# All 64x64 products of a step together on TensorE, in a fixed order, with the outputs of a unit one step later

## The chip, the cores and the metric

The kernel runs on one core of one Trainium2 chip. The metric is the device time of one execution in microseconds. A ratio is the mean time of one kernel's fast runs over the mean of the other's fast runs of the same rounds on the same chip, so it is not quite the ratio of the medians that stand beside it.

## The reference

An mLSTM cell, then a multiplicative feed-forward network (FFN), all in fp32. There are 4 batches, 8 heads, 768 steps and a head size of 40. Its recurrence is

```python
C = f_stab * C + i_stab * outer(v_t, k_t);  n = f_stab * n + i_stab * k_t
y_t = sigmoid(o_t) * (C @ q_t) / max(|n . q_t|, 1)
# bridge: x is y as (3072, 320)
out = ((x @ w1) * (x @ w2)) @ w3 @ w_out        # 320 -> 1024 -> 1024 -> 320
```

Both kernels compute the recurrence in blocks. A *unit* is one batch and 128 time steps, that is two halves of 64 steps; there are 24 units. They also fold `w3 @ w_out` into one matrix `w3o` on the way, and convert the weights, which come as 64-bit words, on VectorE.

## The kernel before

For each unit TensorE makes these products (names as in the profile):

- `pt`: k and q transposed, 128x128 transposes that use the full array. ScalarE copies them to `kT` and `qT`.
- `ss`: scores of a half; `pc`: what a half adds to the state; `pi`: what the state gives to the outputs; `ph`: weighted scores times v. These use 64 rows and 64 columns of the array, so up to four run side by side in its quarters.
- `px`: y transposed to `xT`, the input of the FFN.

The FFN has `pa` and `pb` (x times w1 and w2). Its 320 input columns are two blocks of 128 and a *rest* of 64, and the rests of pa and pb run as two 64x128 products. `po` is the output product. `w3p` and `wp` fold w3.

```python
def scores(n):
    ...
    _, ss = two_banks("ss", L)                 # one PSUM buffer of two banks for ss, pc and pi in turn
    for p in range(NP):
        for hip, x in ((0, 0), (1, 1), (0, 1), (1, 0)):
            nc.tensor.matmul(ss[t, hip, p, :], lhsT=kT[r, p, t], rhs=qT[r, p, t], ...)
    nc.vector.tensor_tensor(out=pv, in0=ss, in1=pv, op=OP.mult)          # pw
def cell(n):                                   # one step after scores(n)
    ...                                        # pc; two states; pi; h; ph; h; den; o_in; y
    nc.gpsimd.tensor_copy(out=y_t[n][:, DM:DM + REM], in_=y_t[n][:, KF * P:DM])
for s in ...:                                  # program order; the scheduler may move instructions
    turn(s)                                    # pt
    ffn_up(first); scores(s); convert(...); cell(s - 1)
    ffn_up(others); x_trans(s - 2); ffn_out(...)          # px stands near the end of the step
```

The scheduler that builds the instruction streams may change the order of independent products on TensorE, and does.

## Time and profile before

| | before |
|---|---|
| median, fastest, slowest | 549.59, 548.06, 551.09 us (4 runs) |
| profiled span | 545.3 us |
| mean granted TensorE clock (share of full speed) | 0.978 |
| TensorE busy | 92% |

### The profile page before, as it was taken

The page shows a single profiled execution, that of the slowest core. Times are in us where ns is not written, and L with a number is a line of the kernel's source. Part 1 is how long each engine was busy: PE and PEld are TensorE (multiplying, and loading weights), DVE is VectorE, ACT ScalarE, POOL GpSimd, SP SyncE. Part 2 cuts the span into 40 slices and gives each one's busy share as a digit, 9 for nine tenths or more (in the row PEclk, how much of TensorE's full clock was granted, in tenths as well). Part 3 has the DMA queues.
Part 4 walks back from the last instruction along what each step waited for, and adds up shares of the span by engine and source line. Part 5 has one row for each costly group of instructions (what it writes and reads, how often), then busy time and mean ns, then how long its engine had stood idle before and what let it go on. Part 6 is the DMA issues. An engine that isn't in the chain of part 4 may idle for free.

```text
span 545.3 us, 11006 instructions
## 1 busy us (share of the span) xinstructions
PE 500.7 (92%) x4538; PEld 302.7 (56%) x4538; DVE 231.9 (43%) x500; ACT 174.2 (32%) x419; POOL 88.0 (16%) x157
## 2 busy tenths in 40 slices
PE   4647989896999998999989999999999999999997
PEld 3535666674555554555556665556555455353675
DVE  7856779895655654655613202331232100101000
ACT  3636655854343154143153213212110111111100
POOL 2432343241212212212101302200000000000000
PEclk9966999999999999999989999999999999999999
DMA  8698999987224355222232213200000000000011
GB/s 172 134 168 187 172 198 178 199 203 167 63 72 133 85 99 133 70 66 57 37 69 57 68 39 68 44 13 14 13 1 25 0 24 25 0 24 1 24 37 37
DMA packets 113042, 43.32 MB, mean 79 GB/s; under 512 B 102304, under 2 KB 105504, under 8 KB 112992
## 3 DMA queue, kind: packets, MB, share of 16 engines
q1 hardware_dynamic: 112992, 42.61, 35.8%
q8 instruction: 36, 0.59, 0.5%
q14 instruction: 14, 0.11, 0.1%
HBM read 38.57 MB, written 4.03 MB: 78 GB/s over the span
## 4 chain that ended last, share of the span: by engine, by line
PE 68%; DVE 2%; ACT 2%; DMA 2%; issue 2%; SPq 0%; POOL 0%; DVEq 0%; ACTq 0%; POOLq 0%
PE po L435 19%; PE pa L424 13%; PE pb L424 12%; PE pa L427 7%; PE wp L209 7%; PE ph L291 2%; PE pc L263 2%; PE pt L231 2%; PE pi L284 2%; PE px L314 1%; DVE pw L244 1%; PE ss L242 1%; ACT a_sb L429 1%; DMA raw<-in_moe_w_dram 1%; DMA pw<-U_rest 1%
## 5 line engine op out<-in xcount | busy, mean ns | idle before, releaser
L430 DVE TENSOR_TENSOR ab<-pb,a_sb 128x512 f32<-128x512 f32 (+1 forms) x56 | 34.3, 613 | 204.3 <-ACT a_sb L429 135.6
L435 PE MATMUL po<-w3o,ab 128*128 128x320 f32 x384 | 105.8, 433 | 0.0
L424 PE MATMUL pa<-xT,w 128*128 128x512 f32 (+1 forms) x224 | 99.4, 557 | 3.6 <-ACT xT L315 3.6
L424 PE MATMUL pb<-xT,w 128*128 128x512 f32 (+1 forms) x224 | 94.4, 541 | 0.5 <-DVE w L153 0.5
L435 PEld LDWEIGHTS po<-w3o,ab 128*128 128x128 f32 x384 | 72.0, 190 | 30.1 <-issue 1.5
L222 ACT ACTIVATE pw<-pw,aT 128x64 f32<-128x64 f32 x192 | 52.9, 341 | 55.7 <-DMA pw<-U_rest 42.5
L429 ACT ACTIVATE a_sb<-pa 128x512 f32<-128x512 f32 (+1 forms) x56 | 29.8, 532 | 126.8 <-PE pb L427 125.4
L424 PEld LDWEIGHTS pb<-xT,w 128*128 128x128 f32 x224 | 41.5, 191 | 36.1 <-issue 32.3
L427 PE MATMUL pa<-xT,wr 64*128 64x512 f32 (+1 forms) x112 | 56.0, 580 | 0.2 <-DVE wr L153 0.2
L427 PE MATMUL pb<-xT,wr 64*128 64x512 f32 (+1 forms) x112 | 56.0, 580 | 0.0
L424 PEld LDWEIGHTS pa<-xT,w 128*128 128x128 f32 x224 | 37.5, 190 | 30.8 <-issue 23.9
L258 POOL TENSOR_TENSOR vw<-vbuf,wT 128x328 f32<-128x328 f32 x24 | 22.1, 920 | 156.7 <-PE pc L263 87.3
L224 POOL TENSOR_SCALAR_AFFINE_SELECT pw<-pw 64x512 f32<-64x512 f32 x48 | 34.4, 718 | 59.3 <-ACT pw L222 57.7
L438 ACT COPY o_sb<-po 128x320 f32<-128x320 f32 x24 | 10.2, 426 | 87.1 <-PE po L435 84.5
L209 PE MATMUL wp<-wo,w3T 128*128 128x320 f32 x128 | 37.7, 449 | 0.3
L427 PEld LDWEIGHTS pa<-xT,wr 64*128 64x128 f32 x112 | 16.5, 184 | 35.3 <-issue 34.7
L209 PEld LDWEIGHTS wp<-wo,w3T 128*128 128x128 f32 x128 | 24.3, 195 | 10.5 <-DVE w3T L203 1.1
L291 PE MATMUL ph<-vbuf,pw 64*64 64x41 f32 x768 | 29.9, 233 | 0.0
L291 PEld LDWEIGHTS ph<-vbuf,pw 64*64 64x64 f32 x768 | 27.3, 142 | 1.6 <-issue 0.5
L263 PEld LDWEIGHTS pc<-vw,kbuf 64*64 64x64 f32 x704 | 15.5, 146 | 21.9 <-DVE pw L244 15.9
L148 ACT ACTIVATE raw<-raw 128x512 f32<-128x512 f32 (+1 forms) x34 | 21.4, 631 | 19.6 <-DMA raw<-in_moe_w_dram 19.6
L263 PE MATMUL pc<-vw,kbuf 64*64 64x41 f32 x704 | 19.3, 242 | 8.3 <-DVE pw L244 8.3
(78 smaller groups left out, 503.4 us busy)
## 6 DMA issues: line engine op xcount, KB each, us to landing
raw<-in_moe_w_dram SPq DMA_DIRECT2D x24, 512.0 KB, 4.6
pw<-U_rest SPq DMA_DIRECT2D x40, 128.0 KB, 3.7
kbuf<-in_k_dram SPq DMA_DIRECT2D x24, 160.0 KB, 4.2
qbuf<-in_q_dram SPq DMA_DIRECT2D x24, 160.0 KB, 4.4
vbuf<-in_v_dram SPq DMA_DIRECT2D x24, 160.0 KB, 3.8
o_in<-in_o_gate_dram SPq DMA_DIRECT2D x24, 160.0 KB, 3.7
out_dram<-o_sb SPq DMA_DIRECT2D x24, 160.0 KB, 1.8
raw<-in_moe_w_out_dram SPq DMA_DIRECT2D x8, 320.0 KB, 4.0
```

The costliest lines, as they stand in the source:

```text
L148: nc.scalar.mul(out=hi.bitcast(FP), in_=hi.bitcast(FP), mul=2.0 ** -111)
L209: nc.tensor.matmul(wp, lhsT=w3T[:, ki, :], rhs=wo[:, ki, :], start=(ki == 0), stop=(ki == FO - 1))
L222: nc.scalar.activation(out=pw[:, h, :], in_=pw[:, h, :], func=AF.Exp, bias=aT[:, c, b * H + h:b * H + h + 1])
L224: nc.gpsimd.affine_select(out=pw[r], in_=pw[r], compare_op=OP.is_ge, fill=0.0, base=0, pattern=[[0, H], [1, L]], channel_multiplier=-1)
L258: nc.gpsimd.tensor_tensor(out=vw, in0=vt, in1=wT[:, c, hs].unsqueeze(2).to_broadcast([P, H, D1]), op=OP.mult)
L263: nc.tensor.matmul(pc[halves[e], x, p, :], lhsT=kt[halves[x], 2 * p + e, :], rhs=vw[halves[x], 2 * p + e, :], start=True, stop=True)
L291: nc.tensor.matmul(ph[r, hd, :], lhsT=pw[r, hd, :], rhs=vt[r, hd, :], start=True, stop=True)
L424: nc.tensor.matmul(p, lhsT=wt[:, cc, fs], rhs=pick(x[:, cc, :]), start=(cc == 0), stop=False)
L427: nc.tensor.matmul(p, lhsT=wr[r, fs], rhs=pick(x[r, KF, :]), start=False, stop=True)
L429: nc.scalar.mul(out=a_sb, in_=pa, mul=UP ** -2)
L430: nc.vector.tensor_tensor(out=pick(ab), in0=pb, in1=a_sb, op=OP.mult)
L435: nc.tensor.matmul(po, lhsT=ab_t[gr][:, f, j * P:(j + 1) * P], rhs=w3o[:, f, :], start=(f == 0), stop=(f == FO - 1))
```

## The change

The intent: the products in quarters of the array stand together once a step, so that the array changes its shape rarely; TensorE keeps a given order; the rests of the FFN's blocks run in quarters too, in the same *stay* (one stretch of TensorE in one shape of the array); a unit's h and y come a step after its scores, so that no product of the cell waits inside a unit; PSUM, the memory that takes TensorE's products, is divided into four rotating banks and one cell buffer of four banks. The core of the diff, with cuts:

```diff
+    def in_order(ins):                        # each product depends on the one before it
+        if last:
+            tc.add_manual_dep(ins.ins, last.pop().name, ...)
...
-    ps_t bufs=3; ps_s bufs=1 (two banks); ps_m bufs=3
+    ps_m bufs=4; ps_c bufs=1 (four banks)
...
+    def quarter_work(s, rest):
+        rest()                                # rests of pa and pb as four 64x64 products
+        t = ps_c.tile([P, 4, 512], FP, name="cell", tag="cell")
+        ...                                   # ph and pi of unit s-1, then pc and ss of unit s
+            first_read = nc.vector.tensor_tensor(out=pv, in0=ss, in1=pv, op=OP.mult)     # pw
+            with tc.issue_after(first_read.ins):
+                ...                           # the two states
+        if 0 <= s - 1 < NU:
+                with tc.issue_after(first_read.ins):
+                    outputs(s - 1, pi, ph)    # h, den, o_in, y, copy of y's tail
...
     for s in range(len(n_up)):
+            weights(s + 1); weighted(s); decayed(...)
             turn(s)
+        if 0 <= s - 2 < NU:
+            x_trans(s - 2)                    # px, now right behind pt
+        fold()
+        for _ in range(n_down[s]):
+            ffn_out(*downs.pop(0))
+        open_ups = [up(*x) for x in now[:2]]
+        quarter_work(s, rest)
-        if 0 <= s - 2 < NU:
-            x_trans(s - 2)                    # behind all products of the step
```

More of the change, by code (lines that the diff above doesn't have):

```diff
@@ L69, with mm, transpose @@
     dram = ctx.enter_context(tc.tile_pool(name="dram", bufs=1, space=bass.MemoryType.DRAM))
-    ps_t = ctx.enter_context(tc.tile_pool(name="ps_t", bufs=3, space=bass.MemoryType.PSUM))
-    ps_s = ctx.enter_context(tc.tile_pool(name="ps_s", bufs=1, space=bass.MemoryType.PSUM))
-    ps_m = ctx.enter_context(tc.tile_pool(name="ps_m", bufs=3, space=bass.MemoryType.PSUM))
-    def tps(shape, name):
-        return ps_t.tile(shape, FP, name=name, tag="t")
-    def mps(shape, name):
-        return ps_m.tile(shape, FP, name=name, tag="m")
-    def two_banks(name, n):
-        t = ps_s.tile([P, 2, 512], FP, name=name, tag="s")
-        return t, t[:, :, 0:NP * n].rearrange("p x (n d) -> p x n d", d=n)
+    ps_m = ctx.enter_context(tc.tile_pool(name="ps_m", bufs=4, space=bass.MemoryType.PSUM))
+    cell_psum = ExitStack()
+    ps_c = cell_psum.enter_context(tc.tile_pool(name="ps_c", bufs=1, space=bass.MemoryType.PSUM))
+    banks = [ps_m]
+    def mps(shape, name):
+        pool = banks.pop(0)
+        banks.append(pool)
+        return pool.tile(shape, FP, name=name, tag="m")
+    last = []
+    def in_order(ins):
+        if last:
+            tc.add_manual_dep(ins.ins, last.pop().name, mybir.DependencyInfo(
+                mybir.DependencyClass.NoSync, mybir.DependencyReason.DATA), reason="in_order")
+        last.append(ins.ins)
+    def mm(out, lhsT, rhs, start=True, stop=True):
+        in_order(nc.tensor.matmul(out, lhsT=lhsT, rhs=rhs, start=start, stop=stop))
+    def transpose(out, in_):
+        in_order(nc.tensor.transpose(out, in_, ident))
     halves = [slice(0, L), slice(L, P)]
+    quarters = ((0, 0), (1, 1), (0, 1), (1, 0))
     NB, NBQ = 4, 3
@@ L177, in fetch @@
         pend.append((dst, raw_tile(dst.shape[-1] if dst is not None else CW, pieces), i, part))
+    later = []
     def convert():
@@ L183, in convert, with fold @@
             to_f32(dst, raw)
-            w3_trans(dst, ko, half)
+            later.append((dst, ko, half))
+        else:
+            to_f32(dst, raw)
+    def fold():
+        while later:
+            w3, ko, half = later.pop(0)
+            w3_trans(w3, ko, half)
             if half:
                 w3_mm(ko)
-        else:
-            to_f32(dst, raw)
     w3T_t = {}
@@ L195, in w3_trans @@
             w3T_t[ko] = wst.tile([128, FO, 128], FP, name="w3T", tag="w3T")
-        tp = tps([128, FO // 2, 128], "w3p")
+        tp = mps([128, FO // 2, 128], "w3p")
         for j in range(FO // 2):
-            nc.tensor.transpose(tp[:, j, :], w3[:, j * 128:(j + 1) * 128], ident)
+            transpose(tp[:, j, :], w3[:, j * 128:(j + 1) * 128])
         r = slice(half * (FO // 2), (half + 1) * (FO // 2))
@@ L208, in w3_mm @@
         for ki in range(FO):
-            nc.tensor.matmul(wp, lhsT=w3T[:, ki, :], rhs=wo[:, ki, :], start=(ki == 0), stop=(ki == FO - 1))
+            mm(wp, w3T[:, ki, :], wo[:, ki, :], start=(ki == 0), stop=(ki == FO - 1))
         nc.scalar.mul(out=w3o[:, ko, :], in_=wp, mul=UP ** -2)
-    qT_t, kT_t, y_t, x_t = {}, {}, {}, {}
+    qT_t, kT_t, vw_t, before_t, y_t, x_t = {}, {}, {}, {}, {}, {}
     def out_gate(gr):
@@ L228, in turn @@
         for src, dst, name in ((kbuf[n % NB], kT_t, "kT"), (qbuf[n % NBQ], qT_t, "qT")):
-            pt = tps([128, NP, P], "pt")
+            pt = mps([128, NP, P], "pt")
             for p in range(NP):
-                nc.tensor.transpose(pt[:, p, :], src[:, 2 * p:2 * p + 2, :].rearrange("p a b -> p (a b)"),
-                                    ident)
+                transpose(pt[:, p, :], src[:, 2 * p:2 * p + 2, :].rearrange("p a b -> p (a b)"))
             dst[n] = sb.tile([128, NP, P], FP, name=name, tag=name)
@@ L234, in turn @@
             nc.scalar.copy(out=dst[n], in_=pt)
-    def scores(n):
-        kT, qT, pw = kT_t.pop(n), qT_t[n], u_t[n]
-        _, ss = two_banks("ss", L)
-        for p in range(NP):
-            for hip, x in ((0, 0), (1, 1), (0, 1), (1, 0)):
-                r, t = halves[hip], halves[x]
-                nc.tensor.matmul(ss[t, hip, p, :], lhsT=kT[r, p, t], rhs=qT[r, p, t], start=True, stop=True)
-        pv = pw.rearrange("p (n two) t -> p two n t", two=2)
-        nc.vector.tensor_tensor(out=pv, in0=ss, in1=pv, op=OP.mult)
@@ L246, in cell @@
-    def cell(n):
-        c, b = divmod(n, B)
-        pw, vt, kt = u_t.pop(n), vbuf[n % NB], kbuf[n % NB]
-        qT = qT_t.pop(n)
-        first, second, after = state[b]
-        state[b] = after, second, first
-        hs = slice(b * H, (b + 1) * H)
-        quarters = ((0, 0), (1, 1), (0, 1), (1, 0))
-        ends = range(2 if c < NT2 - 1 else 1)
-        vw = sb.tile([P, H, D1], FP, name="vw", tag="vw")
-        nc.gpsimd.tensor_tensor(out=vw, in0=vt, in1=wT[:, c, hs].unsqueeze(2).to_broadcast([P, H, D1]), op=OP.mult)
-        _, pc = two_banks("pc", D1)
-        for p in range(NP):
-            for x, e in quarters:
-                if x in ends:
-                    nc.tensor.matmul(pc[halves[e], x, p, :], lhsT=kt[halves[x], 2 * p + e, :],
-                                     rhs=vw[halves[x], 2 * p + e, :], start=True, stop=True)
-        def next_state(new, old, x):
-            c1 = 2 * c + x - (2 if c else 0)
-            if (c, x) > (0, 0):
-                nc.gpsimd.tensor_tensor(out=new, in0=old, op=OP.mult,
-                                        in1=dec_of[min(c, 1)][:, b * NP:(b + 1) * NP, c1:c1 + 1]
-                                        .to_broadcast([P, NP, D1]))
-                nc.vector.tensor_tensor(out=new, in0=pc[:, x], in1=new, op=OP.add)
-            else:
-                nc.vector.tensor_copy(out=new, in_=pc[:, x])
-        next_state(second, first, 0)
-        if len(ends) > 1:
-            next_state(after, second, 1)
-        h = sb.tile([P, H, D1], FP, name="h", tag="h")
-        _, pi = two_banks("pi", D1)
-        for p in range(NP):
-            for hip, x in quarters:
-                r, t = halves[hip], halves[x]
-                nc.tensor.matmul(pi[t, hip, p, :], lhsT=qT[r, p, t], rhs=(first, second)[x][r, p, :], start=True, stop=True)
@@ new lines, in weighted, with decayed @@
+    def weighted(n):
+        c, b = divmod(n, B)
+        vw_t[n] = sb.tile([P, H, D1], FP, name="vw", tag="vw")
+        nc.gpsimd.tensor_tensor(out=vw_t[n], in0=vbuf[n % NB], op=OP.mult,
+                                in1=wT[:, c, b * H:(b + 1) * H].unsqueeze(2).to_broadcast([P, H, D1]))
+    def decayed(new, old, n, x):
+        c, b = divmod(n, B)
+        c1 = 2 * c + x - (2 if c else 0)
+        nc.gpsimd.tensor_tensor(out=new, in0=old, op=OP.mult,
+                                in1=dec_of[min(c, 1)][:, b * NP:(b + 1) * NP, c1:c1 + 1].to_broadcast([P, NP, D1]))
@@ new lines, in quarter_work, with part @@
+    def quarter_work(s, rest):
+        rest()
+        t = ps_c.tile([P, 4, 512], FP, name="cell", tag="cell")
+        def part(j, c0, n):
+            return t[:, j:j + 2, c0:c0 + NP * n].rearrange("p x (n d) -> p x n d", d=n)
+        ss, pc, pi = part(0, 0, L), part(0, NP * L, D1), part(2, 0, D1)
+        ph = [t[halves[x], 2 + x, NP * D1:(NP + H) * D1].rearrange("p (h d) -> p h d", d=D1) for x in range(2)]
+        n = s - 1
+        if 0 <= n < NU:
+            pw, vt, qT = u_t.pop(n), vbuf[n % NB], qT_t.pop(n)
+            before = before_t.pop(n)
+            for hd in range(H):
+                for x, r in enumerate(halves):
+                    mm(ph[x][:, hd, :], pw[r, hd, :], vt[r, hd, :])
+            for p in range(NP):
+                for hip, x in quarters:
+                    mm(pi[halves[x], hip, p, :], qT[halves[hip], p, halves[x]], before[x][halves[hip], p, :])
+        n, first_read = s, None
+        if n < NU:
+            c, b = divmod(n, B)
+            kt, vw = kbuf[n % NB], vw_t.pop(n)
+            ends = range(2 if c < NT2 - 1 else 1)
+            first, second, after = state[b]
+            before_t[n] = first, second
+            state[b] = after, second, first
+            for p in range(NP):
+                for x, e in quarters:
+                    if x in ends:
+                        mm(pc[halves[e], x, p, :], kt[halves[x], 2 * p + e, :], vw[halves[x], 2 * p + e, :])
+            kT, qT, pw = kT_t.pop(n), qT_t[n], u_t[n]
+            for p in range(NP):
+                for hip, x in quarters:
+                    mm(ss[halves[x], hip, p, :], kT[halves[hip], p, halves[x]], qT[halves[hip], p, halves[x]])
+            pv = pw.rearrange("p (n two) t -> p two n t", two=2)
+            first_read = nc.vector.tensor_tensor(out=pv, in0=ss, in1=pv, op=OP.mult)
+            with tc.issue_after(first_read.ins):
+                if c:
+                    nc.vector.tensor_tensor(out=second, in0=pc[:, 0], in1=second, op=OP.add)
+                else:
+                    nc.vector.tensor_copy(out=second, in_=pc[:, 0])
+                if len(ends) > 1:
+                    decayed(after, second, n, 1)
+                    nc.vector.tensor_tensor(out=after, in0=pc[:, 1], in1=after, op=OP.add)
+        if 0 <= s - 1 < NU:
+            if first_read is None:
+                outputs(s - 1, pi, ph)
+            else:
+                with tc.issue_after(first_read.ins):
+                    outputs(s - 1, pi, ph)
@@ L285, in cell, with outputs @@
+    def outputs(n, pi, ph):
+        c, b = divmod(n, B)
+        hs = slice(b * H, (b + 1) * H)
+        h = sb.tile([P, H, D1], FP, name="h", tag="h")
         nc.vector.tensor_tensor(out=h.rearrange("p (n two) d -> p two n d", two=2), in0=pi,
@@ L287, in cell @@
                                 .to_broadcast([P, 2, NP, D1]), op=OP.mult)
-        ph = tps([P, H, D1], "ph")
-        for hd in range(H):
-            for r in halves:
-                nc.tensor.matmul(ph[r, hd, :], lhsT=pw[r, hd, :], rhs=vt[r, hd, :], start=True, stop=True)
-        nc.vector.tensor_tensor(out=h, in0=ph, in1=h, op=OP.add)
+        for x, r in enumerate(halves):
+            nc.vector.tensor_tensor(out=h[r], in0=ph[x], in1=h[r], op=OP.add)
         den = sb.tile([P, H, 1], FP, name="den", tag="den")
@@ L311, in x_trans @@
         y = y_t.pop(n)
-        px = tps([128, KF + 1, P], "px")
+        px = mps([128, KF + 1, P], "px")
         for cc in range(KF + 1):
-            nc.tensor.transpose(px[:, cc, :], y[:, cc * P:(cc + 1) * P], ident)
+            transpose(px[:, cc, :], y[:, cc * P:(cc + 1) * P])
         nc.scalar.copy(out=x_t[gr][:, :, j * P:(j + 1) * P], in_=px)
@@ L345, in gate_cols @@
         def gate_cols(src, dst, c0, c1):
-            pg = tps([P, c1 - c0, BH], "pg")
+            pg = mps([P, c1 - c0, BH], "pg")
             for c in range(c0, c1):
@@ L393, in first_units @@
             load_u(2)
-            for u in range(2):
-                weights(u)
-                turn(u)
+            weights(0)
             convert()
@@ L409, with up, up_rest @@
     ab_t = {}
-    def ffn_up(gr, f, part):
-        if f == 0 and part in (None, 0):
+    def up(gr, fs, cs):
+        if gr not in ab_t:
             ab_t[gr] = ffn.tile([128, FO, TG], FP, name="ab", tag="ab", bufs=3)
-        x, fs, ab = x_t[gr], slice(f * 128, (f + 1) * 128), ab_t[gr][:, f, :]
-        n = TG if part is None else TG // 2
-        def pick(t):
-            return t if part is None else t[:, part * n:(part + 1) * n]
-        pa, pb = mps([128, n], "pa"), mps([128, n], "pb")
-        for p, wt in ((pa, w1), (pb, w2)):
-            for cc in range(KF):
-                nc.tensor.matmul(p, lhsT=wt[:, cc, fs], rhs=pick(x[:, cc, :]), start=(cc == 0), stop=False)
-        for j, p in enumerate((pa, pb)):
-            r = slice(j * REM, (j + 1) * REM)
-            nc.tensor.matmul(p, lhsT=wr[r, fs], rhs=pick(x[r, KF, :]), start=False, stop=True)
-        a_sb = ffn.tile([128, TG], FP, name="a_sb", tag="a_sb")[:, 0:n]
+        x, n = x_t[gr], cs.stop - cs.start
+        pa, pb = mps([128, len(fs), n], "pa"), mps([128, len(fs), n], "pb")
+        for p, wt in ((pa, w1), (pb, w2)):
+            for i, f in enumerate(fs):
+                for cc in range(KF):
+                    mm(p[:, i, :], wt[:, cc, f * 128:(f + 1) * 128], x[:, cc, cs], start=(i == cc == 0), stop=False)
+        return pa, pb, x, gr, fs, cs
+    def up_rest(pa, pb, x, gr, fs, cs):
+        for i, f in enumerate(fs):
+            for j, e in quarters:
+                mm((pa, pb)[j][halves[e], i, :], wr[halves[j], f * 128 + e * L:f * 128 + (e + 1) * L],
+                   x[halves[j], KF, cs], start=False, stop=(i == len(fs) - 1))
+        a_sb = ffn.tile([128, len(fs), cs.stop - cs.start], FP, name="a_sb", tag="a_sb")
         nc.scalar.mul(out=a_sb, in_=pa, mul=UP ** -2)
-        nc.vector.tensor_tensor(out=pick(ab), in0=pb, in1=a_sb, op=OP.mult)
+        nc.vector.tensor_tensor(out=ab_t[gr][:, fs[0]:fs[-1] + 1, cs], in0=pb, in1=a_sb, op=OP.mult)
     def ffn_out(gr, j):
@@ L434, in ffn_out @@
         for f in range(FO):
-            nc.tensor.matmul(po, lhsT=ab_t[gr][:, f, j * P:(j + 1) * P], rhs=w3o[:, f, :],
-                             start=(f == 0), stop=(f == FO - 1))
+            mm(po, ab_t[gr][:, f, j * P:(j + 1) * P], w3o[:, f, :], start=(f == 0), stop=(f == FO - 1))
         o_sb = ffn.tile([P, DM], FP, name="o_sb", tag="o_sb", bufs=3)
@@ L440, in ffn_out @@
         nc.sync.dma_start(out=out[t0:t0 + P, :], in_=o_sb)
-    ups = [(0, f, part) for part in range(2) for f in range(FO)]
-    ups += [(gr, f, None) for gr in range(1, NG) for f in range(FO)]
+    ups = [(0, list(range(f, f + 4)), slice(j * P, (j + 1) * P)) for f in (0, 4) for j in range(2)]
+    ups += [(0, [f, f + 1], slice(2 * P, 4 * P)) for f in range(0, FO, 2)]
+    ups += [(gr, [f], slice(0, TG)) for gr in range(1, NG) for f in range(FO)]
     downs = [(gr, j) for gr in range(NG) for j in range(GT)]
-    n_up = [0] * 4 + [4, 0, 3, 3, 3, 3] + [2] * 8 + [0] + [2] * 5 + [4, 2, 4, 4]
-    n_down = [0] * 18 + [4, 1, 1, 1, 1, 2, 2, 2, 2, 2, 2, 4]
+    n_up = [0, 0, 1, 1, 0, 2, 2, 1, 1] + [2] * 17 + [2, 2, 2, 0]
+    n_down = [0] * 16 + [2, 2] + [1] * 8 + [2, 3, 3, 4]
     w12 = [("w12", i, part) for part in range(2) for i in range(2 * KF + 1)]
-    fold = [("wo", i, 0) for i in range(FO)] + [("w3", ko, part) for ko in range(FO) for part in range(2)]
-    todo = w12[3:] + fold
-    n_cvt = [2, 1, 1, 1, 2, 2] + [2] * 12
-    for s in range(max(len(n_up), len(n_down))):
+    todo = w12[3:] + [("wo", i, 0) for i in range(FO)] + [("w3", ko, part) for ko in range(FO) for part in range(2)]
+    n_cvt = [2, 2, 2, 2, 1, 2, 2, 3, 3] + [2] * 7
+    for s in range(len(n_up)):
         if 3 <= s + 2 < NU:
@@ L458, with rest @@
             load_o(s + GT)
-        if 2 <= s < NU:
-            weights(s)
-            turn(s)
-        now = [ups.pop(0) for _ in range(n_up[s] if s < len(n_up) else 0)]
-        for x in now[:1]:
-            ffn_up(*x)
-        if s < NU:
-            scores(s)
+        if s + 1 < NU:
+            weights(s + 1)
+        if s < NU:
+            weighted(s)
+            if s >= B:
+                decayed(state[s % B][1], state[s % B][0], s, 0)
+            turn(s)
+        if 0 <= s - 2 < NU:
[3 more added lines that the diff above has]
+            ffn_out(*downs.pop(0))
+        now = [ups.pop(0) for _ in range(n_up[s])]
+        open_ups = [up(*x) for x in now[:2]]
+        def rest():
+            for x in open_ups:
+                up_rest(*x)
+        if s <= NU:
+            quarter_work(s, rest)
+        else:
+            rest()
+        if s == NU:
+            cell_psum.close()
+            banks.append(ctx.enter_context(tc.tile_pool(name="ps_x", bufs=4, space=bass.MemoryType.PSUM)))
         for _ in range(n_cvt[s] if s < len(n_cvt) else 0):
@@ L472 @@
             out_gate(0)
-        if 0 <= s - 1 < NU:
-            cell(s - 1)
         if s % GT == GT - 1 and s + 1 < NU:
             out_gate(s // GT + 1)
-        for x in now[1:]:
-            ffn_up(*x)
-        if 0 <= s - 2 < NU:
-            x_trans(s - 2)
-        for _ in range(n_down[s] if s < len(n_down) else 0):
-            ffn_out(*downs.pop(0))
-    assert not ups and not downs and not todo and not pend
+    assert not ups and not downs and not todo and not pend and not later, (len(ups), len(downs), len(todo), len(pend))
 _INS = ['q', 'k', 'v', 'i_gate', 'f_gate', 'o_gate', 'moe_w1', 'moe_w2', 'moe_w3', 'moe_w_out']
```

## The prediction

> **What bounds the kernel now.** I read the page first (engines and slices), then busy time by stretch, then TensorE's instructions in order of time in one steady step, then the list of waits.
>
> ```profile
> PE 500.7 (92%) x4538; PEld 302.7 (56%) x4538; DVE 231.9 (43%) x500; ACT 174.2 (32%) x419; POOL 88.0 (16%) x157
> PE   4647989896999998999989999999999999999997
> DVE  7856779895655654655613202331232100101000
> ```
>
> TensorE carries the span, except in the first ten slices or so (to about 135 us), where VectorE shows 7 to 9 tenths. The stretches say the same with numbers:
>
> ```profile
> 0.00:60.00 60.00, 35.64 (x562) 28.64 (x563) 41.68 (x92) 28.40 (x70) 20.09 (x44) 0.83 0.85 164
> 60.00:140.00 80.00, 69.65 (x991) 49.06 (x990) 63.77 (x151) 50.32 (x124) 26.54 (x41) 1.00 0.85 180
> 140.00:300.00 160.00, 153.53 (x1520) 89.36 (x1519) 85.14 (x171) 56.50 (x135) 27.99 (x46) 0.99 0.36 80
> ```
>
> Columns: stretch, length, busy PE, weight loads, DVE, ACT, POOL, then clock, DMA share, GB/s. Before 140 us VectorE converts weights nearly without a pause and the DMA engines are 85% busy; after it VectorE is half idle and TensorE is alone. But a busy TensorE is not an efficient one. One step:
>
> ```profile
> 337.62 1.88 PE L424 MATMUL pa<-xT,w 128*128 128x512 f32 x4
> 339.34 1.88 PE L424 MATMUL pb<-xT,w 128*128 128x512 f32 x4
> 341.15 0.69 PE L427 MATMUL pa<-xT,wr 64*128 64x512 f32 x1
> ...
> 342.21 0.69 PE L242 MATMUL ss<-qT,kT 64*64 64x64 f32 x32
> 342.73 1.08 PE L291 MATMUL ph<-vbuf,pw 64*64 64x41 f32 x32
> 343.74 1.12 PE L424 MATMUL pa<-xT,w 128*128 128x512 f32 x2
> 344.79 0.68 PE L263 MATMUL pc<-vw,kbuf 64*64 64x41 f32 x32
> 345.40 1.13 PE L424 MATMUL pa<-xT,w 128*128 128x512 f32 x2
> 346.36 1.02 PE L424 MATMUL pb<-xT,w 128*128 128x512 f32 x2
> 347.31 0.68 PE L284 MATMUL pi<-state,qT 64*64 64x41 f32 x32
> 347.92 1.13 PE L424 MATMUL pb<-xT,w 128*128 128x512 f32 x2
> ```
>
> Columns: start, length, operation, rows*columns of the array in use, shape, count (an fp32 product is two records). Read differences of starts. Four 512-wide records in a row take 339.34-337.62 = 1.72 us, 0.43 each. The four before 64x128 work take 341.15-339.34 = 1.81: leaving the full array costs 0.09. The 64x128 visit takes 342.21-341.15 = 1.06 where its two pairs would stream in 0.86: 0.20 more. Two full records between two visits take 344.79-343.74 = 1.05 instead of 0.86: 0.19 more. A visit of pc or pi takes 0.61; where two such groups follow each other with no change of shape (three cases in the trace) it is 0.46, so 0.15 more. A round trip from the full array to quarters and back costs about 0.15 + 0.19 = 0.34 us, and this step makes three besides the 64x128 visit.
>
> I sorted all matmul starts by array shape. The streaming times (0.43, 0.27, 0.22, 0.11 us for 512, 320, 256, 128 columns, 0.058 for four quarters of a cell product or two of ph) sum to 437 us. There are 247 changes of shape; the typical excess of each kind, added up, is 43 us, 0.17 a change. The rest of the span is waits, some 65 us, most of them before 140 us.
>
> ```profile
> PE pi L284 <- DVE state L272: 9.2, 9, 2.8
> PE pc L263 <- DVE pw L244: 8.3, 12, 1.9
> ```
>
> Columns: who waited for whom, us in all, times, longest. The cell products wait for VectorE inside a unit, since ss, pc and pi share one PSUM buffer.
>
> **What the Trainium skill says.** "TensorEngine Tiling (Array Packing)", Key Properties: changing the tiling mode drains the engine, changing only the tile doesn't. The trace agrees: 0.15 to 0.2 us at each change, and none between pi and another quarter group. "TensorE: Matmul & The Clock Gate", Part 3: small tiles overlap at about 4 ns each. The trace gives 0.46 us for 32 records of 41 columns, 14 ns each, so four do run side by side. The first page's Gotcha 1: different row tiles must write different PSUM banks. That explains the split of ph over two banks; no trace here shows the collision itself.
>
> **The change, part by part.**
> (1) One stay in quarters per step. Steps 0 to 24 make one each, four later steps have one for the rests alone: 29 stays, 58 changes instead of 247. At 0.17 that is 10 us instead of 43: 33 less. Of the 247 changes, 83 lie before 139 us, where VectorE and DMA set the pace; their 14 us are mostly not on the path. Gain that counts: 164 changes x 0.17 = 28, less 20 later stays x 0.34 = 7, so 21 us.
> (2) Rests in quarters: four 64x64 products replace two of 64x128. A quarter pass of four streams like a pair: same 0.86 us at 512 columns, without its own 0.29 of mode change (counted in 1).
> (3) Outputs one step later, one cell buffer of four banks: the pi and pc waits inside a unit go, up to 17 us; about half of them lies after 140 us, so 8.
> (4) VectorE gets one more h addition a unit (each half of ph alone, still 328 wide): 24 x 0.50 = 12 us, more work only where VectorE binds: 9 units early, about 4 us.
> (5) The fixed order takes away fillers. Before, pc stood between the weight transposes and wp; now wp follows at once and waits for VectorE's and ScalarE's copy of w3T (0.68 and 0.58 us). ScalarE has eight exponentials (341 ns each) and the copy of xT ahead of it. My estimate is 1.2 us a fold, 8 folds: 10 us; 2 to 4 us elsewhere.
> (6) Banks: four rotate for everything else. A step with eight products goes round twice. The two held-open products free theirs (0.59 ACT, 0.69 DVE) while TensorE spends 2.3 us on the quarters: no wait expected.
>
> Now the sum by stages. The new program does by the end of step 8 what the old did by step 9 less one unit, with 20 weight conversions against 17. VectorE must do until then: gates 12, conversions 10 x 3.0 + 8 x 2.2 + 2 x 3.0 = 54, cell 8.5 x 4.4 = 37, ab 8 x 0.69 = 6, so 109. In the old run its busy time by 131 us, where step 10 began (first transpose at 131.4), was 105, and 26 idle. The cell's round trips are fewer now, so I take 22 idle: step 9 begins at 131.
> From step 9 on, by streaming: steps 9 to 15, each 0.87 (pt) + 0.33 (px) + 0.87 (w3p) + 4.3 (wp) + 6.86 (two ups) + 1.72 (rests) + 2.3 (cell) = 17.3, seven of them 121; step 16 with two po of 4.3, 26; step 17, 21; six steps of 16.4, 98; the last six, 105. In all 371. Add 7 for 20 stays, 4 for the tail, as now, and 12 for waits: 394. 131 + 394 = 525; I round down a little for a shorter early stage: 524 us.
>
> **Rivals.**
> A: VectorE and DMA take the gain back. If the early stage is set by transfers (DMA share 0.85) and the 12 us of extra VectorE work counts, step 9 starts at 142 and the end is 536. For it: VectorE ran nearly without a pause from 85 to 131 us. Against: it idled 15 us between 20 and 60 us on the cell's round trips, which get shorter.
> B: the fixed order stalls TensorE at banks or at xT, say 1 us in each of 21 steps more: 545, no gain. For it: four banks serve six kinds of tile, and ScalarE's copies stand behind exponentials. Against: most steps have 4.3 us of po or wp between the transposes and their use.
> C: all waits of the cell vanish early as well; step 9 at 120 and waits of 6: 507. For it: the fillers are larger; against: the conversions alone hold VectorE.
>
> **Range and chances.** The later stage is counted from measured spacings, to about 6 us; the early stage is good to 9 us, and the stalls of the fixed order to 6. Together some 12: 510 to 537. Within 2% means above 537.9. Faster by over 2%: 0.88; within 2%: 0.10; slower: 0.02.
>
> **What would show each step.** (1) TensorE in the steady steps: one quarter stay each, about 58 changes in all, PE records 2 passes x the same columns. (2) four quarter records of a rest starting within some 20 ns, 0.86 to 1.0 us a rest. (3) no wait of TensorE for state or pw. (5) waits of wp for w3T, about 10 us. (6) no wait of pt or pa for a copy longer than 0.5 us. Early stage: first w3p at about 133 us. I'd be wrong if that came after 142 us, if quarter rests took over 1.2 us each, or if waits after step 9 summed to over 25 us.

## More of the kernel before

One line of its slices is wanted later: the granted clock of TensorE in 40 equal slices, in tenths of full speed.

```profile
PEclk9966999999999999999989999999999999999999
```

Only the two slices from 27 to 55 us are low, so in most of this run TensorE keeps its full clock. The profile has no record of the clock before 27 us; there four transposes took 1.11 us (at 6.74 us) against 0.60 us later (at 69.46 us), so the clock was probably half there too.

## The result

The changed kernel takes 684.77 us (683.23 to 688.17, 4 runs) against 549.59 us. The ratio is 1.2468 (95% interval 1.2408 to 1.2529). The prediction said 524, and that it would be faster.

The page of the changed kernel: the busy line, then two rows of slices and the clock.

```profile
PE 515.7 (76%) x4890; PEld 336.7 (49%) x4890; DVE 245.4 (36%) x516; ACT 178.5 (26%) x411; POOL 81.6 (12%) x157
PE   0574555856778769679579787886888889799998
DVE  8569797233554434634430303203203320200000
PEclk9976768877789779689798988977987898899999
```

TensorE is now idle in part of nearly every slice, also where VectorE is far from full, and its clock is low in many slices. The mean granted clock is 0.872 instead of 0.978. TensorE's busy time went up by 15 us although its streaming work is the same and the array changes its shape less often: part of the work ran at half clock.

The list of waits says for what TensorE waits (columns: who for whom, us in all, times, longest):

```profile
PE px L93 <- DVE y L340: 115.2, 24, 9.6
...
PE px L93 <- POOL y L342: 24.5, 12, 3.0
```

In the kernel before, px waits for y once:

```profile
PE px L314 <- DVE y L303: 1.8, 1, 1.8
```

In the changed kernel px, the transpose of y, waits 139.7 us. One step in order of time shows how. First TensorE, from the end of its stay in quarters (columns as in the prediction, in brackets the idle time before and what ended it):

```profile
386.54 0.66 PE L90 MATMUL cell<-qT,kT 64*64 64x64 f32 x30
387.13 0.66 PE L93 MATMUL pt<-ident,kbuf 128*128 128x128 f32 x4
387.63 0.60 PE L93 MATMUL pt<-ident,qbuf 128*128 128x128 f32 x4
392.41 0.66 PE L93 MATMUL px<-ident,y 128*128 128x128 f32 x2 [4.18 <-DVE y L340]
395.67 0.48 PE L93 MATMUL px<-ident,y 128*128 128x128 f32 x1 [2.61 <-POOL y L342]
395.94 10.12 PE L90 MATMUL po<-w3o,ab 128*128 128x320 f32 x32
```

Then VectorE in the same stretch, cut to five of its ten rows:

```profile
387.29 0.69 DVE L304 TENSOR_TENSOR pw<-cell,pw 128x512 f32<-128x512 f32 x1 [1.03 <-PE cell L90]
...
388.79 0.33 DVE L313 TENSOR_TENSOR state<-cell,state 128x164 f32<-128x164 f32 x1 [0.58 <-POOL state L263]
389.03 0.49 DVE L325 TENSOR_TENSOR h<-cell,gT 128x328 f32<-128x328 f32 x1
389.55 1.01 DVE L329 TENSOR_TENSOR h<-cell,h 64x328 f32<-64x328 f32 x2
...
391.77 0.49 DVE L340 TENSOR_TENSOR y<-h,o_in 128x320 f32<-128x320 f32 x1
```

VectorE can start only when `ss`, the last product of the stay, is done (387.29). It makes pw, two states with a round over POOL between them, h in three pieces, den, o_in and then y, which is ready at 392.26. But in the fixed order px stands right behind the transposes, 0.9 us after the stay. So TensorE stands still while 8.6 us of output products and 6.9 us of FFN products, which need nothing of this, stand behind px in its queue. A second chain ends later still: px's third transpose reads the copy of y's tail, which POOL makes behind two masks, and these behind eight exponentials on ScalarE. The exponentials here wait for the DMA of their input:

```profile
391.86 2.02 ACT L241 ACTIVATE pw<-pw,aT 128x64 f32<-128x64 f32 x8 [2.96 <-DMA pw<-U_rest]
...
393.95 1.37 POOL L243 TENSOR_SCALAR_AFFINE_SELECT pw<-pw 64x512 f32<-64x512 f32 x2 [5.19 <-ACT pw L241]
395.38 0.24 POOL L342 COPY y<-y 128x64 f32<-128x64 f32 x1
```

To put the whole in sums, I took all starts of matmuls in each trace and split the distance from one start to the next into the streaming time of the first (0.43 us for 512 columns and so on, as in the prediction) and the excess. Excess of over 0.7 us at once counts as a wait, excess while the profile's record has the granted clock at half counts as slow clock, and the remainder is mostly changes of shape. The last two columns belong to experiments below.

| us | before | changed | px_next | fill |
|---|---|---|---|---|
| streaming | 437 | 437 | 437 | 562 |
| changes of shape (number) | 249 | 59 | 61 | 59 |
| remainder of the excess | 55 | 15 | 18 | 24 |
| waits over 0.7 us | 36 | 166 | 50 | 53 |
| slow clock | 8 | 55 | 14 | 10 |
| time granted half clock | 24 | 175 | 35 | 24 |

The change did what it was made for: 190 changes of shape fewer, and 40 us less of that excess. It lost 130 us in waits and 47 us to the clock. 40 gained and 177 lost are the 137 us by which the span grew (545.3 to 682.5). The first weight transpose came 176 us after the start, 140 in the kernel before.

### The profile page after: what moved, and what is told of

Read it like the earlier page. It is cut to its first block, busy times and chain, and to the rows that moved or that the text cites. A ratio compares the mean times of both kernels' runs of the same rounds, so it can differ in the third digit from the quotient of the medians.

```text
span 682.5 us, 11729 instructions
## 1 busy us (share of the span) xinstructions
PE 515.7 (76%) x4890; PEld 336.7 (49%) x4890; DVE 245.4 (36%) x516; ACT 178.5 (26%) x411; POOL 81.6 (12%) x157
## 4 chain that ended last, share of the span: by engine, by line
PE 61%; issue 10%; DMA 7%; DVE 6%; POOL 3%; SPq 1%; ACT 0%; POOLq 0%; DVEq 0%; ACTq 0%
PE pa L90 18%; PE po L90 18%; PE pb L90 11%; PE wp L90 7%; DMA pw<-U_rest 6%; PE cell L90 4%; POOL pw L243 2%; PE w3p L93 2%; PE px L93 2%; DVE h L329 1%; DVE pw L304 1%; SPq L120 1%; DVE o_in L338 1%; DVE y L340 1%; DVE h L325 1%
## 5 line engine op out<-in xcount | busy, mean ns | idle before, releaser
L466 DVE TENSOR_TENSOR ab<-pb,a_sb 128x512 f32<-128x512 f32 x48 | 33.2, 691 | 335.7 <-ACT a_sb L465 332.1
L93 PE MATMUL px<-ident,y 128*128 128x128 f32 x72 | 22.8, 413 | 139.7 <-DVE y L340 115.2
L90 PE MATMUL pa<-xT,w 128*128 128x512 f32 (+2 forms) x256 | 100.7, 537 | 1.1 <-ACT xT L352 1.1
L90 PE MATMUL pb<-xT,w 128*128 128x512 f32 (+2 forms) x256 | 91.7, 492 | 0.0
L465 ACT ACTIVATE a_sb<-pa 128x512 f32<-128x512 f32 x48 | 28.5, 597 | 159.2 <-PE pb L90 159.2
L263 POOL TENSOR_TENSOR state<-state,dec 128x164 f32<-128x164 f32 x40 | 19.3, 482 | 296.4 <-PE cell L90 275.4
L90 PE MATMUL pa<-xT,wr 64*64 64x512 f32 (+2 forms) x256 | 47.1, 493 | 0.0
L90 PE MATMUL pb<-xT,wr 64*64 64x512 f32 (+2 forms) x256 | 47.1, 493 | 0.0
L473 ACT COPY o_sb<-po 128x320 f32<-128x320 f32 x24 | 10.2, 425 | 104.0 <-PE po L90 104.0
L90 PEld LDWEIGHTS cell<-vbuf,pw 64*64 64x64 f32 x768 | 27.7, 142 | 15.1 <-issue 14.4
L90 PE MATMUL cell<-vbuf,pw 64*64 64x41 f32 x768 | 27.7, 231 | 5.0 <-issue 5.0
```

Of the source, the lines that this page charges most:

```text
L90: in_order(nc.tensor.matmul(out, lhsT=lhsT, rhs=rhs, start=start, stop=stop))
L93: in_order(nc.tensor.transpose(out, in_, ident))
L263: nc.gpsimd.tensor_tensor(out=new, in0=old, op=OP.mult, in1=dec_of[min(c, 1)][:, b * NP:(b + 1) * NP, c1:c1 + 1].to_broadcast([P, NP, D1]))
L465: nc.scalar.mul(out=a_sb, in_=pa, mul=UP ** -2)
L466: nc.vector.tensor_tensor(out=ab_t[gr][:, fs[0]:fs[-1] + 1, cs], in0=pb, in1=a_sb, op=OP.mult)
L473: nc.scalar.copy(out=o_sb, in_=po)
```

## The experiments

The theory to test: the loss is px's place in the fixed order, directly behind the quarters whose VectorE chain makes its operand, and the clock's loss follows from that idle time. Rivals: four rotating banks stall whatever the order is; the deferred outputs and the longer chain on VectorE bind; the clock fell for another reason; a fixed order is bad as such. All kernels below gave correct results.

### px_next: px a step later

```diff
-        if 0 <= s - 2 < NU:
-            x_trans(s - 2)
+        if 0 <= s - 3 < NU:
+            x_trans(s - 3)
-    n_up = [0, 0, 1, 1, 0, 2, 2, 1, 1] + [2] * 17 + [2, 2, 2, 0]
-    n_down = [0] * 16 + [2, 2] + [1] * 8 + [2, 3, 3, 4]
+    n_up = [0, 0, 0, 1, 1, 2, 1, 1, 1, 1] + [2] * 20 + [0]
+    n_down = [0] * 16 + [2, 2] + [1] * 8 + [2, 2, 2, 2, 4]
```

> Only the place of one product is changed: the transpose px of a unit's y goes a whole step later in the fixed order, the FFN's schedule is shifted by a step to match; quarters, fixed order, PSUM split, deferred outputs all stay. Theory (px stands in the fixed order right behind the quarters whose VectorE chain makes its y): TensorE's wait for y falls from 115 us to under 5, the wait for y's copy on POOL from 24 to under 5, the granted clock goes from 0.87 to over 0.96, and the time to 520 to 545 us. Rival 1 (four banks and held-open products stall whatever the order): time stays over 620 with waits on ScalarE's copies. Rival 2 (the deferred outputs and VectorE's longer chain bind): time over 620, with VectorE's chain as the releaser of ph or of the cell buffer.

Measured: 529.82 us against 546.68, ratio 0.968 (0.9643 to 0.9717), clock 0.967. The same rows of TensorE, in a step of this kernel that has a fold:

```profile
158.54 0.66 PE L90 MATMUL cell<-qT,kT 64*64 64x64 f32 x30
159.14 0.66 PE L93 MATMUL pt<-ident,kbuf 128*128 128x128 f32 x4
159.63 0.60 PE L93 MATMUL pt<-ident,qbuf 128*128 128x128 f32 x4
160.06 0.49 PE L93 MATMUL px<-ident,y 128*128 128x128 f32 x3
160.39 1.04 PE L93 MATMUL w3p<-ident,w 128*128 128x128 f32 x8
```

px follows pt with no gap: its y was made a step ago. In the whole run px waits for VectorE's y for 1.3 us:

```profile
PE px L93 <- DVE y L340: 1.3, 2, 0.8
```

So some 155 of the changed kernel's 685 us hang on this one place, and the quarters, the fixed order, the banks and the deferred outputs are all still in this kernel. The FFN's schedule had to move with px by a step; px_mid below keeps that of the changed kernel. The deferred outputs don't bind, and the banks cost little: waits that look like waits for a bank (px for a_sb, pa for ab, w3p and pb for kT) sum to 9.5 us, the longest 1.9 us. The change without the misplaced px is 3.2% faster than the kernel before. By the table it keeps 37 us less of the remainder, and gives back 20 us of that in waits and slow clock.

### fill: useless products in the idle time

```diff
         px = mps([128, KF + 1, P], "px")
+        for _ in range(24):
+            mm(px[:, 0, :], ident, ident)
```

> Adds useless work: 24 products of the identity with itself (0.22 us each at full clock, 5.2 us in all) into px's own bank in front of each px. Theory (about 47 us of the loss is the granted clock, which falls because TensorE idles some 5 us a step): the filler stands where TensorE idled anyway, the clock goes back to over 0.95 and the time falls by 25 to 50 us, to about 640 to 660, although TensorE does 125 us more work. Rival 3 (the clock has nothing to do with the idle time): time rises by the part of the filler that doesn't fit, to 690 or more, and the clock stays at 0.87.

Measured: 659.49 us, ratio 1.2047 (1.2003 to 1.2091), clock 0.982. The granted clock by slices, as above:

```profile
PEclk9898999899999898999999999999999999999999
```

The same kernel with 125 us more work on TensorE is 25 us faster than the change. The time granted half clock fell from 175 to 24 us and the slow-clock term from 55 to 10. The clock's loss is thus a consequence of the pauses in front of px. "TensorE: Matmul & The Clock Gate", "Why this matters for your kernels", says to avoid idle gaps of over about 3 us between bursts of matmuls, or the clock falls to half. Each of the changed kernel's 24 pauses for y, of 3.3 to 9.6 us, has one stretch at half clock of 3.4, 6.8 or 10.2 us, which begins in the pause or within 1.2 us of its end. Part 4 of that page says that transposes don't count as busy for the clock in the same way; fill used ordinary products of the identity, so no run here tests that.

### outputs_first: y sooner, px where it is

```diff
+        if 0 <= s - 1 < NU:
+            outputs(s - 1, pi, ph)            # ahead of pc and ss of unit s
         n, first_read = s, None
...
-        if 0 <= s - 1 < NU:
-            ...  outputs(s - 1, pi, ph)       # behind the scores' reading
```

> The outputs of the last unit are issued on VectorE before the reading of the scores and the states of this unit, no longer after; fixed order and place of px are those of the change. Theory: y is ready some 2.2 us sooner after the quarters (pw 0.68, two states 0.33, a POOL round of 0.9), so the wait for y falls from 115 us to about 50 to 65, that for POOL's copy stays or grows; time 600 to 640. Rival 2 in its strong form (only the chain on VectorE counts, not px's place): under 560.

Measured: 586.01 us, ratio 1.0711 (1.0681 to 1.0741), clock 0.947. This is better than the expected 600 to 640. The waits of TensorE:

```profile
PE cell L90 <- DVE h L325: 50.6, 23, 6.5
...
PE px L93 <- DVE y L336: 8.8, 5, 3.5
```

The wait for y nearly went, but a new one came: pc now waits in the middle of the stay until VectorE has read pi and ph, which lie in the same cell buffer. Together they are 59 us, about half of the change's 115. The distance counts from both ends: a shorter chain helps as a later px does, and this version pays 2 us a unit for it. The wait for POOL's copy, expected to stay or grow, is gone: a step's copy now starts 0.06 us after y (at 349.97 us), no longer behind masks.

### px_mid: px behind the fold or the output products of its step

```diff
-        if 0 <= s - 2 < NU:
-            x_trans(s - 2)
         fold()
         for _ in range(n_down[s]):
             ffn_out(*downs.pop(0))
+        if 0 <= s - 2 < NU:
+            x_trans(s - 2)
```

> The change with its own schedule; px of a unit stands in the same step but behind the weight products (fold, 5.2 us) or the output products (4.3 us each) instead of ahead of them. Theory (the wait is the distance in TensorE time between the quarters and px, against about 5.3 us until y and 8.5 us until POOL's copy of its tail): full waits stay in steps 2 to 8, which have no such filler (some 6 x 5 us), about 1 to 2 us a step later; px waits in all 45 to 75 us against 140, clock 0.90 to 0.95, time 580 to 615. Rival 1 (banks and ScalarE's copies): over 640.

Measured: 590.31 us, ratio 1.0751 (1.068 to 1.0821), clock 0.936.

```profile
PE px L93 <- DVE y L340: 50.1, 13, 8.5
PE px L93 <- POOL y L342: 14.4, 12, 2.7
```

That is 64.5 us instead of 139.7. Only 13 waits for y are left, no longer 24. The wait shrinks with the work put between the stay and px, as the theory has it.

### tail_dve: the copy of y's tail on VectorE

```diff
-        nc.gpsimd.tensor_copy(out=y_t[n][:, DM:DM + REM], in_=y_t[n][:, KF * P:DM])
+        nc.vector.tensor_copy(out=y_t[n][:, DM:DM + REM], in_=y_t[n][:, KF * P:DM])
```

> The change with one instruction moved: the copy of y's last 64 columns goes from POOL, where it stands behind two masks and these behind eight exponentials, to VectorE right behind y. Theory of a second chain: the 24 us that px waits for that copy go, the 115 us for y stay; time 655 to 672. Rival: the wait moves to y or to something else and the time stays within 1% of 685.

Measured: 651.84 us, ratio 1.1861 (1.179 to 1.1932), clock 0.89: 33 us less than the change, a little more than expected.

```profile
PE px L93 <- DVE y L340: 109.8, 23, 8.7
```

The second chain is real, and the first stays as it was.

### free_order: the change without the fixed order

```diff
-        if last:
+        if False:
             tc.add_manual_dep(...)
```

> The change with the dependencies that fix TensorE's order taken out, so that the scheduler orders it as in the kernel before; nothing else. Theory: the scheduler moves px behind other products, the wait for y drops to under 30 us, but the quarters may be torn apart again, with 100 changes of shape or more; time 530 to 580 us. Rival 2 (deferred outputs): over 640 still, as the data come no sooner.

Measured: 601.97 us, ratio 1.1002 (1.0973 to 1.1031), clock 0.901, 115 changes of shape. The wait for y is gone (2.7 us), as expected, but the time is above the expected range. The scheduler put ph and pi of the next step early, right behind the transposes, and there they wait (TensorE's rows, then one of VectorE's):

```profile
302.17 0.60 PE L93 MATMUL pt<-ident,qbuf 128*128 128x128 f32 x4
305.76 1.82 PE L90 MATMUL cell<-vbuf,pw 64*64 64x41 f32 x30 [3.00 <-issue]
```

```profile
304.66 1.01 DVE L329 TENSOR_TENSOR h<-cell,h 64x328 f32<-64x328 f32 x2
```

The profile names no releaser. But ph starts at 305.76, 0.09 us after VectorE's last reading of the cell buffer ended (305.67), and there is only one such buffer. The list of waits has 65.1 us of this kind. So the scheduler swapped one misplaced product for another.

### next_free: px_next without the fixed order

The same edit as in free_order, on px_next.

> px_next without the dependencies that fix TensorE's order. If px's distance is the whole matter, the scheduler has little to move and the time is within 1% of px_next's 530. Rival (the fixed order is needed, as free_order's 602 could be read): over 560, with cell products ahead of the buffer they need.

Measured: 528.86 us, ratio 0.9625 (0.9589 to 0.966), where px_next had 0.968. The two orders differ only in some products of the first 40 us and in one group of pa near 425 us. The fixed order is therefore not needed once the program's own order has no product right behind its operand's maker.

### before_order: the kernel before in program order

```diff
+    def mm(*a, **k):
+        in_order(nc.tensor.matmul(*a, **k))
-    nc.tensor.matmul(...), nc.tensor.transpose(...)
+    mm(...), transpose(...)                   # all but those of the gates
```

> The kernel before with its matmuls and transposes held in program order, nothing else. It has pc, pi and ph of a unit on consecutive lines with VectorE's work between, and px behind all products of the step. If a fixed order costs wherever a product stands right behind its data's maker: waits for pw and state of 3 to 4 us a step, 620 to 680. Rival (the order as such is harmless): within 3% of 549.

Measured: 640.6 us, ratio 1.1663 (1.1615 to 1.1711), clock 0.896.

```profile
PE pi L93 <- DVE state L286: 51.2, 24, 3.7
PE pc L93 <- DVE pw L258: 23.7, 15, 4.9
```

The same disease with other products: pi directly behind the state that VectorE makes, pc behind pw. The kernel before was good because the scheduler filled these places. A fixed order takes that away, and then the distances have to be right by hand.

### rest_apart: each rest in a stay of its own

```diff
-        open_ups = [up(*x) for x in now[:2]]
+        for x in now[:2]:
+            up_rest(*up(*x))
+        open_ups = []
```

on px_next.

> px_next with each rest right behind its own full-array products again, still in quarters of 64x64, so that every one of 48 FFN pieces makes a stay of its own; 61 changes of shape become about 155. Theory of the prediction's first part (0.17 us a change, 0.34 a stay): 48 stays more, most on the path: 12 to 17 us more than px_next, so 542 to 547. Rival (changes of shape cost nothing once TensorE has no waits): within 4 us of px_next's 530.

Measured: 538.15 us, ratio 0.9788 (0.9699 to 0.9878), that is 1.1% more than px_next's 0.968, some 6 us; the profiled spans differ by 7.1. My count was wrong: where a step has two pieces, the second rest still joins the cell's stay, so the trace has 103 changes, not 155. For 42 changes more, 0.17 us each gives 7.1 us, which agrees. The two intervals overlap slightly, and the verdict against the kernel before is unclear at 2%. But early_turn below, which is as fast as px_next, ran in the same rounds as rest_apart, and its slowest run (532.84) is faster than the fastest one here (534.09). The remainder of the excess in the trace, 28 us against 18, points the same way.

### early_turn: the first units' transposes in the prologue

```diff
-            weights(0)
+            for u in range(2):
+                weights(u)
+                turn(u)
```

on px_next, with the same work taken out of steps 0 and 1.

> px_next with the transposes and weights of units 0 and 1 back in the prologue, as in the kernel before. If the late first transpose (20 us after the start, 7 in the kernel before) is on the path that sets the end: 5 to 12 us less than px_next, 518 to 525. Rival (VectorE's conversions set the early stage whatever TensorE does): within 3 us of 530.

Measured: 531.64 us, ratio 0.9663 (0.9598 to 0.9729): no gain over px_next. The first transpose comes 7 us after the start again instead of 20, and the first weight transpose still at 124 (122 in px_next). The early stage does not hang on this.

### w3_early: the fold's transposes ahead of the others

```diff
     def fold():
-        ...  w3_trans(w3, ko, half); if half: w3_mm(ko)
+        while folded:
+            w3_mm(folded.pop(0))
...
+            fold_trans()                      # the w3_trans calls, ahead of turn
             turn(s)
```

on px_next.

> px_next with the eight transposes of a fold ahead of the unit's own transposes and px, so that 1.2 us of other work lies between them and wp. The prediction's fifth part (wp waits for the copies of w3T): px_next shows 8.3 us of it; here under 2 us, time 520 to 526. Rival (the wait moves to a bank or to px): within 3 us of px_next's 530.

Measured: 522.23 us (520.13 to 524.17, 6 runs) against 548.82, ratio 0.9517 (0.9489 to 0.9546). The wp rows of px_next and then of this kernel:

```profile
L90 PE MATMUL wp<-wo,w3T 128*128 128x320 f32 x128 | 42.6, 490 | 8.3 <-DVE w3T L222 7.9 <-ACT w3T L220 0.4
```

```profile
L90 PE MATMUL wp<-wo,w3T 128*128 128x320 f32 x128 | 39.3, 464 | 4.7 <-ACT w3T L226 3.9 <-DVE w3T L228 0.8
```

The 7.9 us for VectorE's copy fell to 0.8. Of the 4.7 left, 3.9 are one single wait, so my "under 2" missed by that. This version beats both kernels, by 4.8% against the kernel before.

## Why the prediction was wrong

Its sum comes out right for a kernel that differs from the changed one in the place of px: px_next, at 530 us, lies inside the range of 510 to 537. That it comes so near to 524 is in part luck. Its step 9 began at 119 us, where 131 was predicted, and the rest took 409 us, where 394 was predicted; about 5 of these 15 us are FFN work that its shifted schedule moved there. The step that failed is the stall term, part (5): "2 to 4 us elsewhere", with rival B's "1 us in each of 21 steps" as the worst case. The runs showed 139.7 us of waits in front of px in its place, 5.8 us a unit on average, and 47 us of clock on top.

How it failed is worth seeing. In part (5) and in rival B the uses of the transposes were checked: kT, qT and xT have other work between. The operand of px itself was not traced. y of unit s-2 is made in step s-1, which sounds like a step of slack. But the outputs follow the *last* product of step s-1's stay, and px is nearly the *first* of step s. In TensorE's own time the two are 0.9 us apart, against a VectorE chain of 5 us. All durations of the chain stood in the profile of before (0.68, 2 x 0.33, 0.50, 2 x 0.50, 0.49, 0.57 and three small ones). The order of the changed kernel was there to read too.

Point by point:

- **(1) Changes of shape.** Right. 59 changes came, 58 were predicted, and my recount of the kernel before is 249, not 247. The remainder of the excess fell by 40 us; 33 were predicted. rest_apart agrees with the price of 0.17 a change.
- **(2) Rests in quarters.** Right. In the changed kernel the rests of two pieces start at 382.94 and the cell's products at 384.71: 0.89 us a piece, where 0.86 to 1.0 was foretold. The four records of a pass start within 20 ns, so "TensorEngine Tiling (Array Packing)", Key Properties, with its independent tiles holds at 512 columns as well.
- **(3) Waits inside a unit.** Right in itself: no product of the cell waits for pw or a state any more. The wait moved to px. The gain counted for it was too large: of the 17 us of these waits before, not half but 4.7 us lay after 140 us.
- **(4) The extra h addition.** Right in size: 48 halves of 496 ns are 23.8 us, where whole ones had 24 of 497. It was counted as work, not as length of the chain that px waits for; it is 0.5 of the 5 us there.
- **(5) The fold.** Right where it could show. In the changed kernel px's pauses give VectorE time and wp waits 0.2 us; in px_next it is 8.3 us, for a predicted 10. The rest of (5) is the failure told above.
- **(6) Banks.** Right in the changed kernel, where no transpose waits for a bank and pa's two waits for xT are 0.6 us each. In px_next, with the same four banks, the waits of up to 1.9 us named above came, 9.5 us in all.
- **The early stage.** Wrong in the changed kernel (first weight transpose at 176 us, 133 predicted) for the same reason as the rest: px waits in steps 2 to 8 too. In px_next it came at 122, earlier than predicted.
- **The clock** was not in the prediction at all. fill shows that it is the second cost of a pause.
- **Two readings of the lines** were loose. VectorE does not show 7 to 9 tenths in all of the first ten slices (three have 5 or 6): before 140 us it is busy for 105 us, and nearly without a pause only from some 85 to 131 us. And the 14 ns set beside the skill's 4 ns is a mean per record, not the distance of two tiles' starts (see the last section); that four run side by side follows all the same.

What stays open: the profile of free_order doesn't name what its cell products wait for. The single buffer is inferred from the times of start and end, not tested with a second one. px_next's waits for banks are read from the releasers and not tested with more banks.

## What to carry to other kernels

When an order is fixed by hand, check for each product how much of that engine's own work lies between the maker's last input and the use; "a step later" in the program may be next to nothing in time. A pause of a few microseconds on TensorE can cost twice, once itself and once as half clock around it: here the waits grew by 130 us and the slow clock by 47. Grouping products of one array shape pays, here some 0.17 us for each change saved, as long as no product then stands right behind the work that makes its operand.

## What the Trainium skill lacked or had wrong

- "TensorEngine Tiling (Array Packing)", Key Properties, says that a change of mode drains the engine but gives no figure. Here, in the kernel before, a change costs 0.17 us on average, and a round trip from the full array to quarters and back 0.34 us.
- "TensorE: Matmul & The Clock Gate", Part 3, gives about 4 ns between the starts of small tiles that run together. Here the four fp32 records of a group start 6 to 7 ns apart (rests of the changed kernel, near 382.94 us; pc of the kernel before, near 344.79 us). With 41 columns one group follows the other after 58 ns, which makes 0.46 us for 32 records.
